# Four sums moved from the end of a run-time choice to behind it, in an attention and mixture-of-experts kernel

## The chip, the cores and the metric

The kernel runs on one core of a Trainium2 chip. The metric is the device time of one execution in microseconds (us), as a median of five runs. The engines are named as in the profile: PE is TensorE, DVE VectorE, ACT ScalarE, POOL GpSimd, SP the engine that issues most DMAs.

## The reference

Attention with 4 batches, 8 heads, 768 positions and head size 64 gives 3072 tokens of 512 numbers. A router then gives each token to one of 8 experts, and each expert applies two matrix products with a ReLU between them:

```python
logits = xn @ en.T / tau
expert_idx = np.argmax(logits, axis=1)
...
for e in range(E):
    mask = expert_idx == e
    if not mask.any():
        continue
    h = np.maximum(x[mask] @ w1[e], 0.0)          # w1[e]: 512 x 1024
    out[mask] = gate_w[mask, None] * (h @ w2[e])  # w2[e]: 1024 x 512
```

All of it is float32. How many tokens an expert gets is known only while the kernel runs.

## The kernel before

The first 190 us or so are attention and routing, which the change does not touch. After them the experts run one after the other, with a first block of 256 tokens (`n.first`) that was started earlier and ends in front of expert 0. The instructions of PE, ACT, DVE, SP and POOL are issued in the order in which the program is written (`manual_schedule`), so the place of a line in the code is its place in each engine's queue.

**The choice.** Each expert has one arm of a run-time switch per possible width (its number of tokens, rounded up to a multiple of 32). At the switch each engine jumps to the arm for the width; at the arm's end it jumps to the code that stands behind the switch and that all arms share. The widths that this input takes can be read from the matmul shapes of the trace: 160 for expert 0, then 320, 512, 320, 352, 384, 480 and 384 for experts 1 to 7. The widest arm, 512, is the last one in the code, so that its end runs straight on into the code behind the switch.

**An arm of experts 1 to 7.** `first_by_seven` makes the first product in seven smaller products of sums and differences instead of eight. For this it needs sums of the tokens (`xsum`, made by `token_sums`, lines L1039 to L1042) and of the weights w1 (`fsum`, made by `first_sums`, L1064 to L1067). The four sums of a kind have the numbers 0 to 3 in a list. Sums for the *next* expert are made on DVE while this expert runs: the first two of w1 and the first two of x between the seven products, the last two of each at the end of the arm. `making` is the list that an arm runs on DVE after its seven products: four sums of the hidden rows (`hsum`, also L1064 to L1067, 128x512), then the last two of x (L1041, L1042, 128x512) and the last two of w1 (L1066, L1067, 128x1024). Beside this PE makes second products of rows beyond the first 256 (L1219 for full tiles of 128 rows, L1232 for a part of 64 or 32).

**Behind the choice.** `choose_next` loads the width after next into registers (L1490) and gives a hint (L1496). `unfinished.pop()()` finishes the expert before: one DVE instruction (L1112; for expert 0 L1029) reads the PSUM tile `work0` and writes `y`. Then `Pair` makes the second product of the first 256 rows, again in seven smaller products of four matmuls, all at L1101. In `pair.begin` PE makes four of them, ACT copies the first (`p1`, L1121), and DVE adds: `u2` and `u3` (L1105), which ACT multiplies with the gates (L1125, L1131). In `pair.end` PE makes the rest. Its first product goes to `work0`, of which there is one, so it waits until DVE has read the old one; ACT reads it as `p5` (L1144); PE makes the `fourth` product; and only then, because it adds to the tile that ACT had to read, the last product. After this PE jumps into the next expert's arm.

```python
self.product(ps, s1, t1)                          # pair.end
nc.scalar.mul(self.p5, ps, self.gate[1])
self.plus(self.part(1, 1), self.p5, self.u3g)
self.fourth()
self.product(ps, s4, self.b[1][1], True)
```

**Weights.** SP issues the 2 MB load of w1 for expert e+2 when expert e no longer needs its own (L167), and that of w2 likewise (L168).

**Expert 0.** Its token numbers come from DRAM (`numbers`, tile `mts`), DVE casts them to integers (`cast`, tile `idss`), POOL gathers the rows with them (`gather_rows`, L985, tile `xg`), PE turns each 128 rows (`turn_row`, L1011, PSUM tile `work`, three buffers), and ACT or DVE copies them from PSUM into `xT` (L1014). Expert 0's own arm has no sums: it uses `first_by_eight` (L1262).

## Time and profile before

| | us |
|---|---|
| median of 5 runs | 523.61 |
| lowest and highest of them | 521.46, 525.12 |
| the profiled execution: time, span | 524.95, 523.2 |

| engine | busy us | share of the span |
|---|---|---|
| PE (matmul) | 497.0 | 95% |
| PEld (weight load) | 410.7 | 78% |
| DVE | 300.2 | 57% |
| ACT | 198.4 | 38% |
| POOL | 145.0 | 28% |

The span is the time from the first to the last instruction of the profiled execution; its granted TensorE clock was 0.992. In the lists below a row of the timeline gives the start in us from the span's start, the duration, the engine, the line, the operation, the tiles written and read, the count, and in brackets how long the engine was idle before and what ended that. In the chain of waits a row gives start, duration and what ran; "issue" is time in which an engine waited for nothing that the profile shows. Jumps, register loads and semaphore waits are not counted as busy, but the trace has records of them.

### The profile page before, as it was taken

To read this page: it belongs to the slowest core of one execution; us is meant where nothing else is said; L and a number is where in the kernel's file an instruction comes from. 1 tells how busy PE (TensorE), PEld (TensorE's weight loads), DVE (VectorE), ACT (ScalarE), POOL (GpSimd) and SP (SyncE) were. 2 spreads that over 40 slices of the span, in tenths; PEclk is the share of its full clock that TensorE was granted. 3 is DMA by queue.
4 is the path that set the end of the run, shared out by engine and by line. 5 is a ranking of instruction groups with operands and counts; after the bars stand their busy time and mean duration, and the time that the engine had idled before them with its cause. 6 is when DMAs were issued, how large, how long until landed. Compare 5 with 4: busy or idle time off the path is not lost.

```text
span 523.2 us, 13705 instructions
## 1 busy us (share of the span) xinstructions
PE 497.0 (95%) x5606; PEld 410.7 (78%) x5606; DVE 300.2 (57%) x597; ACT 198.4 (38%) x498; POOL 145.0 (28%) x169
## 2 busy tenths in 40 slices
PE   7999999999989799999889999999899999999994
PEld 7677787887857688779778579879799689869963
DVE  5746767766775665657535715836835734633531
ACT  4966776776644322313113212312322222311210
POOL 4221121332254335542430034042133040022031
PEclk9999999999999899999999999999999999999998
DMA  9999988899633517883570056246146423001001
GB/s 174 195 185 178 233 230 192 192 236 209 150 77 115 139 34 180 258 298 127 193 264 3 16 206 233 85 169 241 55 181 226 164 80 145 1 25 58 0 22 68
DMA packets 111422, 76.32 MB, mean 146 GB/s; under 512 B 87078, under 2 KB 95270, under 8 KB 111282
## 3 DMA queue, kind: packets, MB, share of 16 engines
q1 hardware_dynamic: 102769, 59.00, 42.2%
q0 software_dynamic: 6912, 15.26, 8.7%
q8 instruction: 63, 1.03, 0.9%
q14 instruction: 78, 0.63, 0.4%
q10 hardware_dynamic: 1600, 0.39, 0.3%
HBM read 61.66 MB, written 17.16 MB: 151 GB/s over the span
## 4 chain that ended last, share of the span: by engine, by line
PE 56%; DVE 7%; issue 5%; POOL 2%; DMA 2%; ACT 1%; DVEq 0%; POOLq 0%
PE big L1286 24%; PE big L1101 10%; PE work L1219 7%; PE work L1101 5%; PE work L1011 2%; PE pa L670 2%; PE big L1262 2%; PE work L1232 1%; PE work L1021 1%; DMA meta<-mt,slot 1%; DMA xg<-x_dram,idss 1%; POOL meta L256 1%; DVE fsum L1066 1%; POOL ss L223 1%; POOL xg L985 1%
## 5 line engine op out<-in xcount | busy, mean ns | idle before, releaser
L492 DVE TENSOR_TENSOR ex<-ex,table 126x768 f32<-126x768 f32 x64 | 60.6, 952 | 38.7 <-ACT ex L485 38.5
L1298 DVE TENSOR_TENSOR hT<-big,hT 128x320 f32<-128x320 f32 (+4 forms) x70 | 39.4, 566 | 49.7 <-PE big L1286 49.5
L1238 POOL DMA_INDIRECT out_dram<-y_arm,tids x17 | 17.9, 1051 | 166.4 <-ACT y_arm L1221 121.4
L1286 PE MATMUL big<-xT,w1t 128*128 128x160 f32 (+4 forms) x336 | 59.5, 330 | 1.6 <-issue 1.5
L485 ACT ACTIVATE ex<-pa 126x384 f32<-126x384 f32 (+1 forms) x128 | 53.3, 477 | 17.1 <-PE pa L479 16.0
L1286 PEld LDWEIGHTS big<-xT,w1t 128*128 128x128 f32 x336 | 54.1, 190 | 4.6 <-issue 2.8
L508 PE MATMUL od<-ex,v 126*64 126x192 f32 (+1 forms) x576 | 46.2, 305 | 0.4 <-DVE ex L492 0.4
L985 POOL DMA_INDIRECT xg<-x_dram,idss x32 | 32.9, 1028 | 45.1 <-PE big L1286 17.4
L508 PEld LDWEIGHTS od<-ex,v 126*64 126x64 f32 x576 | 34.6, 136 | 8.2 <-issue 3.7
L1014 ACT COPY xT<-work 128x256 f32<-128x256 f32 x60 | 19.3, 376 | 57.1 <-PE work L1011 56.7
L256 POOL DMA_INDIRECT meta<-mt,slot x24 | 27.6, 1149 | 43.9 <-DVE rd L552 21.1
L1286 PE MATMUL big<-xsum,fsum 128*128 128x160 f32 (+4 forms) x224 | 39.6, 330 | 0.0
L479 PE MATMUL pa<-qT,kT 64*32 64x128 f32 (+3 forms) x2048 | 38.1, 263 | 0.7 <-issue 0.5
L479 PEld LDWEIGHTS pa<-qT,kT 64*32 64x32 f32 (+1 forms) x2048 | 29.3, 105 | 11.9 <-issue 6.8
L1286 PEld LDWEIGHTS big<-xsum,fsum 128*128 128x128 f32 x224 | 36.1, 190 | 1.1
L1219 PE MATMUL work<-w2t,hT 128*128 128x512 f32 x80 | 35.1, 593 | 0.0
L1101 PE MATMUL big<-wsum,hsum 128*128 128x256 f32 x136 | 31.1, 380 | 0.7 <-DVE idss L1650 0.5
L1300 ACT ACTIVATE hT<-hT 128x320 f32<-128x320 f32 (+4 forms) x42 | 21.6, 533 | 25.1 <-DVE hT L1298 24.9
L429 POOL COPY v<-v 30x896 f32<-30x896 f32 (+1 forms) x15 | 16.4, 1105 | 49.2 <-DMA v<-in_v_dram 29.5
L1101 PEld LDWEIGHTS big<-wsum,hsum 128*128 128x128 f32 x136 | 25.7, 190 | 5.3 <-issue 1.0
L1101 PE MATMUL big<-w2t,hT 128*128 128x256 f32 x112 | 27.7, 385 | 1.4 <-DVE fsum L1066 1.1
L1219 PEld LDWEIGHTS work<-w2t,hT 128*128 128x128 f32 x80 | 15.1, 190 | 17.5 <-issue 17.2
(245 smaller groups left out, 873.2 us busy)
## 6 DMA issues: line engine op xcount, KB each, us to landing
w1t<-in_moe_w_dram SPq DMA_DIRECT2D x6, 2048.0 KB, 8.9
w2t<-in_moe_w_dram SPq DMA_DIRECT2D x6, 2048.0 KB, 10.0
v<-in_v_dram SPq DMA_DIRECT2D x32, 192.0 KB, 4.4
x_dram<-xs SPq DMA_DIRECT2D x23, 256.0 KB, 4.3
k<-in_k_dram SPq DMA_DIRECT2D x28, 192.0 KB, 4.7
q<-in_q_dram SPq DMA_DIRECT2D x28, 192.0 KB, 4.9
w1t<-in_moe_w_dram SPq DMA_DIRECT2D x32, 128.0 KB, 4.3
w2t<-in_moe_w_dram SPq DMA_DIRECT2D x32, 128.0 KB, 4.3
```

The lines of the kernel that those rows point to most:

```text
L256: i = nc.gpsimd.indirect_dma_start(out=k.meta[:], out_offset=bass.IndirectOffsetOnAxis(ap=slot[:, t : t + 1], axis=0), in_=mt[:, t, :], in ...
L479: i = nc.tensor.matmul(u.sp[e][k0:k1, a * n + c0 : a * n + c1], lhsT=t.kT[rows, j, k0:k1], rhs=t.qT[rows, j * BLK + c0 : j * BLK + c1], st ...
L485: nc.scalar.activation(u.ex[:, e], u.sp[e][0:ROWS, 0 : 2 * u.n].rearrange("p (a c) -> p a c", a=2), AF.Exp, scale=k.scale)
L492: nc.vector.tensor_tensor(out=exv, in0=exv, in1=tab[:, :, 0 : u.n // BLK, :], op=ALU.mult)
L508: nc.tensor.matmul(g.od[a][e * D : (e + 1) * D, at : at + c1 - c0], lhsT=g.v[0:ROWS, 2 * a + e, u.j, :], rhs=u.ex[:, e, a, c0:c1], start=f ...
L985: i = k.nc.gpsimd.indirect_dma_start(out=xg[:], out_offset=None, in_=k.x_dram[0 : upto or k.N + 1, :], in_offset=bass.IndirectOffsetOnAxis ...
L1014: copy(out=xT[:, :, a, j * half : (j + 1) * half].rearrange("p c (q i) -> p c q i", i=LACE), in_=laced(ps[:])[:, a])
L1101: self.k.nc.tensor.matmul(ps, lhsT=x[:, f, :], rhs=w[:, f, :], start=f == 0 and not add, stop=True, skip_group_check=True)
L1219: nc.tensor.matmul(ps[:], lhsT=hT[:, f, j * P : (j + 1) * P], rhs=w2[:, f, :], start=i == 0, stop=i == k.NF - 1)
L1286: nc.tensor.matmul(to[f // 2][:, f % 2 * 256 : f % 2 * 256 + h], lhsT=x[:, l, f * P : (f + 1) * P], rhs=y[:, l, 0:h], start=not (add or f ...
L1298: nc.vector.tensor_tensor(out=to, in0=x, in1=z, op=ALU.add)
L1300: nc.scalar.activation(to, to, AF.Relu)
```

## The change

It has three parts.

1. The last two sums of x and of w1 for the next expert leave the end of the arms of experts 1 to 7 (expert 7 has none, since nothing comes after it). They stand behind the switch, after the DVE instruction that finishes the expert before and ahead of `pair.begin`.
2. The turned rows of expert 0 are copied to `xT` by DVE alone. Before, ACT copied tiles 0 and 2, and DVE tiles 1 and 3.
3. The cast of expert 0's row numbers stands behind one more of the four hidden sums of the first block: behind the third instead of the second in the order in which they are issued.

```diff
@@ expert
         if now.e:
             coming.first_sums, ahead = first_sums(k, coming.w[0])
-            making += more[2:] + ahead[2:]
...
         choose_next()
         out += unfinished.pop()()
+        for make in more[2:] + ahead[2:]:
+            make()
         pair.begin()
@@ kernel
             making[1]()
             making[2]()
+            making[0]()
             cast(0, 1)
             coming = prepare(0)
             gathers = coming.gathers
-            making[0]()
             making[3]()
...
             for j in range(CAP // P):
-                turn_row(n, coming.rows, coming.xT, j, (nc.scalar.copy, nc.vector.tensor_copy)[j % 2])
+                turn_row(n, coming.rows, coming.xT, j, nc.vector.tensor_copy)
```

## The prediction

> **What bounds the kernel now.** I read the chain of waits first. By engine it says that PE sets the time:

> ```profile
> PE 56%; DVE 7%; issue 5%; POOL 2%; DMA 2%; ACT 1%; DVEq 0%; POOLq 0%
> ```

> So a change on DVE counts only where DVE or "issue" stands in the chain. I went through the experts in order of time. Behind experts 2, 4, 5 and 6 the chain is PE alone; behind experts 1 and 3 it leaves PE. This is the chain over the end of expert 1:

> ```profile
> 247.48 0.69 DVE hsum L1064
> ...
> 249.53 0.69 DVE hsum L1067
> 250.22 0.61 DVE xsum L1041
> ...
> 252.76 0.07 DVE fsum L1067
> 252.83 4.25 issue
> ...
> 257.93 0.76 DVE y L1029
> 258.69 0.04 issue
> 258.74 1.99 PE work L1101 x8
> 260.73 1.73 PE big L1101 x8
> 262.46 1.73 PE work L1101 x8
> 264.19 1.53 issue
> ```

> The reader is to see the eight sums at the arm's end, a gap of 4.25 us, then the `y` that frees `work0`, and PE behind it. The four sums that move end at 253.98 and take 3.84 us (250.14 to 253.98). The gap is DVE's jump out of the arm. The trace's record of that jump starts with the last sum, at 252.77, and the next instruction follows 4.30 us later; register work takes another 0.86 us. The list of waits prices the two places for PE:

> ```profile
> PE work L1101 <- DVE y L1029: 1.6, 1, 1.6
> PE work L1101 <- DVE y L1112: 1.3, 1, 1.3
> ```

> These 1.6 us (expert 1) and 1.3 us (expert 3) are all that an earlier `y` can give; every other gap of PE has another cause.

> Next, why the jump is long. Between its record and the next instruction, DVE's jump out of an arm took 4.30, 0.52, 4.26, 5.49, 2.87, 2.74 and 2.73 us behind experts 1 to 7; ACT's took 5.67, 0.40, 5.35, 5.63, 2.57, 2.40 and 2.55. The 0.5 belongs to the last arm, which runs straight on. The quiet price is 2.7. The long ones lie in the load of w1, issued at 248.36, 336.77 and 375.88. The stages view shows DMA share and GB/s in its last two columns:

> ```profile
> 247.00:249.00 2.00, 2.00 (x22) 1.30 (x20) 1.49 (x3) 0.45 (x1) 0.00 (x0) 1.00 0.03 8
> 250.00:251.00 1.00, 1.00 (x7) 0.90 (x6) 0.96 (x3) 0.47 (x1) 0.13 (x1) 1.00 0.87 303
> 251.00:255.00 4.00, 4.00 (x20) 3.53 (x19) 2.95 (x3) 0.00 (x0) 3.28 (x3) 1.00 1.03 421
> 256.00:258.00 2.00, 1.12 (x6) 0.64 (x4) 0.07 (x1) 0.37 (x1) 0.17 (x1) 1.00 0.04 11
> ```

> The load fills the DMA engines from 250 to 255, and the queue view of 249 to 258 has code in it:

> ```profile
> q14 instruction: 4, 0.03, 1.0%
> ```

> I read a jump as a fetch of code that comes behind the load. ACT jumps at 250.13, right as the load starts, and pays 5.67; DVE jumps at 252.77, halfway through, and pays 4.30.

> **Part 1, expert 1.** Without the four sums DVE's jump starts with its last hidden sum, at 249.53 instead of 252.77: 3.24 us earlier, but at the load's start. How long it is there the trace does not show for DVE. Bounds: 2.7 (quiet) and 5.7 (ACT, 0.6 us later in the same stage). I take 5.6, from ACT's row, as the nearest in time. Then DVE is back at 255.13, `y` starts at 255.99 (+0.86), and the sums, which now stand in front of `u2`, run from 256.66 (+0.67) to 260.50 (+3.84). `u2` started at 258.60; it is 1.90 late. PE gains first: it is free at 257.13, finds `work0` read, and no longer waits 1.6. But its last product waits for `p5`, and on ACT `p5` is queued behind the gate products of `u2` and `u3`: from `u2`'s start to `p5`'s end is 0.45 + 0.53 + 0.53 + 0.47 = 1.98 at best. So `p5` ends at 262.48; it ended at 261.24. PE's jump to expert 2 comes 0.35 after `p5` and takes 3.9 us here, past the last product (that is the 1.53 "issue" above). All 1.24 us arrive in expert 2: **+1.24**. In general `p5` ends at 256.88 plus the jump, not before 259.63 (PE's own first product), so the break-even jump is 4.36.

> **Part 1, expert 3.** The jump starts at 337.97 instead of 341.21; load issued 1.2 us before, as for expert 1. I take 5.4 (ACT here 5.35, DVE behind expert 4 5.49). Back at 343.37, `y` 344.23, sums 344.63 to 348.47, `u2` +1.75, `p5` ends 350.45. Here PE's jump is covered, so the end of `p5` counts against the last product's start at 350.58: 0.15 for the semaphore gives 350.60, so nothing, or **+0.1** with the pipeline refilled. The 1.3 us that `y` gives is eaten. Break-even jump: 5.38; PE's own products let at most 1.56 be gained.

> **Part 1, elsewhere.** Expert 4: DVE jumps at 373.95, ahead of its load; with a jump up to 6.1 `p5` still comes from PE. Expert 5: jump at 413.29, in its load; `p5` would end 420.49 plus the jump, against 426.29 now: covered up to 5.8. Experts 2 and 6: DVE idled 8.9 and 6.0 us in front of `u2`. In the built program L1042 and L1067 now also wait for PE's arm to be nearly or wholly done; for experts 2 and 6 that puts the sums' end near 307 and 467.5, before `u2` at 309.36 and 469.97. Zero for all four; without that cover up to 2.4 us each. What needs the sums, the next arm's second product, is over 5 us away. The scatters on POOL only move earlier. [...]

> **Part 2.** Four more DVE copies of 0.38 us and four fewer on ACT. These rows show the place, with part 3's cast and gather:

> ```profile
> 195.39 0.17 DVE L1650 CAST idss<-mts 128x8 int32<-128x8 f32 x1
> 195.47 0.68 DVE L1064 TENSOR_TENSOR hsum<-fhT 128x512 f32<-128x512 f32 x1
> ...
> 195.83 1.19 POOL L985 DMA_INDIRECT xg<-x_dram,idss  x1 [7.72 <-DVE idss L1650]
> ...
> 204.59 0.63 PE L1011 MATMUL work<-ident,xg 128*128 128x128 f32 x4 [0.53 <-DMA xg<-x_dram,idss]
> ```

> DVE is free at 203.33, after a step of the first block, and would copy tiles 0 to 2 by 205.6; PE needs tiles 0 and 1 for expert 0's 160 columns, at 205.60, and tile 0's buffer for the last turning. Tiles 0 and 1 are there at 204.85. DVE's following small steps move by some 0.4 us; it idles 4.97 before the next row that PE's result ends (224.03). **Zero**; at most 0.4 if the cover were gone.

> **Part 3.** The title says three sums; in the built order the cast passes one, L1064, which takes DVE 0.60 us (195.47 to 196.07). POOL had waited for this cast, each gather moves with it, and PE waits 0.53 for the last one. Behind it PE runs through to expert 1 without a break, so **+0.60** arrives. The bound below is 0: the numbers had landed just when the cast ran, and in an execution where they land 0.6 later the sum costs nothing. The sums that passed the cast were not waited for.

> **The sum.** 1.24 + 0.1 + 0.60 = +1.94. Against the profiled 524.95 (span 523.2 and 1.75 around it) this is 526.9; that execution lay 1.34 above the median, so against 523.61 it is **525.6**, or +0.4%. About 0.5%, 2.6 us, is what a measurement of this kernel can tell from no change: my forecast is a small loss inside it.

> **Rival B, not slower: the fetch stays ahead of the load.** At 249.53 and 337.97 the DMA share is still below full (0.29 in 249 to 250). With today's 4.3 us `p5` ends 0.06 earlier at expert 1 and PE's last product starts 1.12 earlier at expert 3: -1.18 + 0.60 = -0.6, or 523.0. With the quiet 2.7 both stages gain what PE allows, 1.61 and 1.56: -3.17 + 0.60, or 521.0. For it: DVE jumps 0.6 us before ACT. Against it: ACT jumped 0.45 us after the load's issue at expert 4, earlier than DVE would (1.2), and paid 5.63.

> **Rival C, slower: the load, not the jump's start, sets when code arrives.** If DVE comes back no earlier than today (257.07, 345.47), `p5` ends 3.2 later at expert 1 and PE's last product starts 2.1 later at expert 3: +5.3 + 0.60, or 529.5. Every us beyond the jumps I took costs 2 us, so half of that mechanism gives 527.5; from jumps 0.35 us longer than taken it is a loss that can be told. For it: DVE's fetch would stand beside ACT's, and the three jumps near 5.5 end when the load is mostly through. Against it: ACT came back at 255.80, earlier than DVE, in the same load.

> **Chances.** The forecast 0.6, with its own range 524.4 to 526.8 (jumps of 5.2 to 5.9, the cast 0 to 0.6); B 0.16; C 0.24. Over 526.2 lie C and about a third of the forecast: slower 0.44. Under 521.0 lies the far end of B: 0.05. Within: 0.51. The range takes in most of B and the half of C: 522.2 to 528.0.

> **What would show it.** Behind experts 1 and 3 DVE's jump starts with L1067 of `hsum` and lasts over 5 us; PE no longer waits for `y`, but for `p5` on ACT, by 1 us or more; L1286 of expert 2 starts later by 1.2 relative to expert 1's start. The last gather of expert 0 lands 0.6 later, and PE's wait for it grows to about 1.1. Jumps under 4.4 and 5.4 would prove B, jumps over 6 C. A new wait behind experts 2, 4, 5 or 6 would make the covers wrong.

## The result and the profile after

The changed kernel takes 525.86 us (median of 39 runs; 522.39 to 528.70) against 523.25 for the kernel before (65 runs). The ratio is 1.0047, with an interval of 1.0035 to 1.0058: a loss of about 2.5 us, small but clear of no change. The forecast was 525.6. The two kernels were compared once more later, where the ratio was 1.0030 (1.0005 to 1.0056).

The profiled execution of the changed kernel took 523.99 us, with a span of 522.2 and a clock of 0.989. It is shorter than that of before, and this has nothing to do with the change: its attention part, which both kernels share, ended 2.1 us earlier (first hidden sum at 191.90 instead of 194.04). From the first hidden sum to the end it took 330.28 us against 329.20, so +1.08. For this reason stages are compared here, not spans. A stage runs from one expert's first product to the next one's; "front" runs from the first hidden sum to expert 0's first product. "Again" is a second profiled execution, from the later comparison, us:

| | front | 0 | 1 | 2 | 3 | 4 | 5 | 6 | 7 | end |
|---|---|---|---|---|---|---|---|---|---|---|
| before | 11.56 | 23.60 | 36.51 | 52.01 | 34.43 | 37.79 | 39.14 | 49.26 | 37.66 | 7.24 |
| before, again | 11.62 | 24.47 | 37.68 | 52.01 | 34.49 | 38.08 | 39.14 | 49.26 | 37.66 | 7.22 |
| after | 12.12 | 23.20 | 37.48 | 52.01 | 34.48 | 37.54 | 39.14 | 49.26 | 37.66 | 7.39 |
| after, again | 12.20 | 24.85 | 37.93 | 52.01 | 34.62 | 37.94 | 39.14 | 49.26 | 37.66 | 7.44 |

Of the +1.08, front brings +0.56, expert 1 +0.97, expert 0 -0.40, expert 4 -0.25, and the rest +0.20.

The list of waits of the kernel after, PE's part from 185 us on, shows the exchange (us in total, times, longest):

```profile
PE work L1101 <- ACT ptmp L1144: 3.3, 2, 1.9
PE work L1011 <- DMA xg<-x_dram,idss: 1.0, 1, 1.0
```

No wait for `y` is left. In its place stand two waits for `p5`, 1.9 behind expert 1 and 1.4 behind expert 3, where the waits for `y` had been 1.6 and 1.3. This is the timeline of the same two places:

```profile
247.47 0.69 DVE L1067 TENSOR_TENSOR hsum<-hT,hsum 128x512 f32<-128x512 f32 x1
254.28 0.75 DVE L1029 TENSOR_SCALAR y<-work,mts 128x512 f32<-128x512 f32 x1 [6.11 <-issue]
254.94 0.68 DVE L1041 TENSOR_TENSOR xsum<-xT 128x512 f32<-128x512 f32 x1
...
257.66 1.22 DVE L1067 TENSOR_TENSOR fsum<-w1t,fsum 128x1024 f32<-128x1024 f32 x1
258.80 0.94 DVE L1105 TENSOR_TENSOR ptmp<-big,ptmp 128x256 f32<-128x256 f32 x2
...
349.36 1.99 PE L1101 MATMUL work<-w2t,hsum 128*128 128x256 f32 x8 [1.36 <-ACT ptmp L1144]
```

DVE leaves the arm right behind its last hidden sum, as the change wants, and then stands idle for 6.11 us. The `y` it returns with is in time; but the four sums now come before `u2` (the row at 258.80), and ACT can make `p5` only behind `u2`. The chain of waits of the kernel after shows where that goes:

```profile
255.08 1.99 PE work L1101 x8
257.07 1.74 PE big L1101 x8
258.81 0.41 DVE ptmp L1105
...
260.19 0.47 ACT ptmp L1144
260.66 0.04 issue
260.70 3.26 PE work L1101 x8
263.96 0.74 issue
264.70 5.42 PE big L1286 x24
```

PE makes its first product as soon as it can, stops, and the chain leaves it for DVE (`u2`) and ACT (`p5`). The windows of DMA traffic (last two columns: DMA share and GB/s) show that the whole jump, from 247.49 to 253.42, lies within the load of w1, which was issued at 246.30 and whose packets run from 247.34 to 254.32:

```profile
249.00:250.00 1.00, 1.00 (x7) 0.87 (x6) 0.00 (x0) 0.00 (x0) 0.83 (x1) 1.00 0.99 410
250.00:255.00 5.00, 5.00 (x24) 4.12 (x22) 0.72 (x2) 0.37 (x1) 2.96 (x3) 1.00 0.77 296
255.00:257.00 2.00, 1.98 (x10) 1.72 (x10) 1.90 (x4) 0.00 (x0) 1.18 (x1) 1.00 0.00 0
```

### The profile page after: what moved, and what is told of

It is laid out like the page before. It is cut to its first block, busy times and chain, and to the rows that moved or that the text cites. A ratio compares the mean times of both kernels' runs of the same rounds, so it can differ in the third digit from the quotient of the medians.

```text
span 522.2 us, 13718 instructions
## 1 busy us (share of the span) xinstructions
PE 498.6 (95%) x5606; PEld 411.3 (79%) x5606; DVE 301.9 (58%) x601; ACT 196.8 (38%) x494; POOL 147.3 (28%) x169
## 3 DMA queue, kind: packets, MB, share of 16 engines
q8 instruction: 63, 1.03, 0.8%
## 4 chain that ended last, share of the span: by engine, by line
PE 82%; DVE 5%; ACT 5%; DMA 3%; issue 2%; POOL 2%; POOLq 0%; SPq 0%; ACTq 0%; DVEq 0%
PE big L1286 25%; PE big L1101 12%; PE work L1219 7%; PE od L508 6%; PE work L1101 5%; PE pa L479 5%; PE work L1232 4%; PE pa L454 3%; PE od L518 3%; PE work L1011 2%; PE pa L670 2%; ACT ex L485 2%; PE big L1262 2%; PE pa L581 1%; PE work L1021 1%
## 5 line engine op out<-in xcount | busy, mean ns | idle before, releaser
L1286 PE MATMUL big<-xT,w1t 128*128 128x160 f32 (+4 forms) x336 | 59.4, 330 | 0.7 <-issue 0.7
L1286 PEld LDWEIGHTS big<-xT,w1t 128*128 128x128 f32 x336 | 54.2, 190 | 3.8 <-issue 1.9
L985 POOL DMA_INDIRECT xg<-x_dram,idss x32 | 33.8, 1055 | 44.1 <-PE big L1286 22.8
L1286 PE MATMUL big<-xsum,fsum 128*128 128x160 f32 (+4 forms) x224 | 39.6, 330 | 0.0
L1014 ACT COPY xT<-work 128x256 f32<-128x256 f32 x56 | 18.0, 376 | 55.7 <-PE work L1011 55.3
L1286 PEld LDWEIGHTS big<-xsum,fsum 128*128 128x128 f32 x224 | 36.1, 190 | 1.1
L1101 PE MATMUL big<-wsum,hsum 128*128 128x256 f32 x136 | 31.1, 380 | 0.5 <-ACT ptmp L1121 0.5
L1101 PEld LDWEIGHTS big<-wsum,hsum 128*128 128x128 f32 x136 | 25.7, 190 | 5.1 <-ACT ptmp L1121 0.9
L1101 PE MATMUL big<-w2t,hT 128*128 128x256 f32 x112 | 27.7, 385 | 1.1 <-ACT y L1234 1.1
```

The costliest lines, as they stand in the source:

```text
L985: i = k.nc.gpsimd.indirect_dma_start(out=xg[:], out_offset=None, in_=k.x_dram[0 : upto or k.N + 1, :], in_offset=bass.IndirectOffsetOnAxis ...
L1101: self.k.nc.tensor.matmul(ps, lhsT=x[:, f, :], rhs=w[:, f, :], start=f == 0 and not add, stop=True, skip_group_check=True)
L1286: nc.tensor.matmul(to[f // 2][:, f % 2 * 256 : f % 2 * 256 + h], lhsT=x[:, l, f * P : (f + 1) * P], rhs=y[:, l, 0:h], start=not (add or f ...
```

## The experiments

**Each part by itself.** Three kernels, each with one part of the change, and one that moves the sums one step further, behind `pair.begin`, so that `u2` comes before them. The edit of the last:

```diff
-            making += more[2:] + ahead[2:]
...
         pair.begin()
+        for make in more[2:] + ahead[2:]:
+            make()
```

Part 1 alone:

> Part 1 alone: the four sums behind the choice, the rest as before. Theory of the prediction (DVE's jump meets the load of w1, and the sums then stand in front of u2 and so of p5): jumps of 5.2 to 5.9 us behind experts 1 and 3, expert 1's stage (its first matmul to expert 2's) +1.0 to +1.25, expert 3's within 0.1, all others 0; time +1.1 to +1.4. Rival (the earlier y wins): jumps under 4.4, time -1 or less. Rival (the moved code itself costs elsewhere, by the layout of DVE's code or by the new waits for PE): other stages grow, time +2 or more.

Part 2 alone:

> Part 2 alone: DVE copies all four of expert 0's turned tiles. Theory: 0.0, PE starts expert 0's first product no later, since tiles 0 and 1 are copied before it is free. Rival (one engine is too slow for four tiles): expert 0's first product starts up to 0.4 later and the time is +0.4. Rival (ACT freed of its copies helps expert 0): the stage of expert 0 is 0.4 shorter, as in the one profile after the change.

Part 3 alone:

> Part 3 alone: the cast of expert 0's row numbers behind one more sum. Theory: +0.6, and PE waits about 1.1 instead of 0.5 us for the last gather of expert 0. Rival (the row numbers land later than the cast in most executions): 0.

Sums behind `pair.begin`:

> The kernel before, with the four sums moved one step further: behind pair.begin, so that y and u2, u3 both come ahead of them. If p5 behind the sums is what eats the gain, then here PE waits neither for y nor for p5: expert 1's stage -1.3 to -1.6 and expert 3's -1.3 to -1.5, time -2.5 to -3.1. Rival (the sums have to be early because the next arm needs them, or DVE's jump into it comes late): PE waits in the next arm instead, and the time is 0 to +2.

Measured, as ratios to the kernel before: part 1 alone 1.0073 (1.0042 to 1.0104), part 2 alone 0.9978 (0.9949 to 1.0008), part 3 alone 0.9996 (0.9967 to 1.0026), sums behind `pair.begin` 0.9929 (0.9893 to 0.9965). So the loss belongs to part 1. It lost some 3.9 us alone, more than the +1.1 to +1.4 of its theory: experts 1 and 3 took 1.16 and 0.18 more, about as expected, but expert 0 took 26.97 instead of 23.60, which is the sign that the second rival had named (taken up again under what stays open). It is not the jump alone that makes the loss: with the same early and long jumps (5.79 and 5.56 us) but `u2` ahead of the sums, the kernel is faster than with part 1 and faster than before. Its stages for experts 1 and 3 took 34.35 and 32.86 us, 2.16 and 1.57 less than before; for expert 1 that is more than the 1.3 to 1.6 expected, because PE's jump into expert 2 came 1.8 earlier, counted from expert 1's start, and took 3.56 us instead of 3.92. The sum, 3.73, is as large as the measured gain (0.71% of 531.45 is 3.8), though front and expert 0 were 2.95 longer in this trace than in that of before. The timeline of this kernel at expert 3 is the counterpart of the one above:

```profile
349.15 0.48 DVE L1112 SCALAR_TENSOR_TENSOR y<-work,mts,u2g 128x256 f32<-128x256 f32 x1 [5.74 <-DMA out_dram<-y_arm,tids]
350.24 0.95 DVE L1105 TENSOR_TENSOR ptmp<-big,ptmp 128x256 f32<-128x256 f32 x2 [0.61 <-issue]
```

`u2` starts 1.1 us after `y`, and PE waits neither for the `y` that frees `work0` nor for `p5`. What is late next is expert 2's first product. PE's list of waits names the adding of the last `y` (L1105), which is now queued behind the sums on DVE; but that `y` ends at 269.75, while PE's own jump, begun at 266.68, has its next instruction at 270.25. So it is PE's jump that holds PE up here, not DVE.

```profile
PE big L1286 <- DVE y L1105: 1.2, 1, 1.2
```

**The two kernels again, half of the move, and the load.** Then came both kernels once more, a kernel in which only the sums of w1 stand behind `pair.begin` and those of x in front of it, and the kernel after with its two loads of weights in the other order, so that w1's load is not under way when DVE jumps:

```diff
         out += unfinished.pop()()
+        for make in more[2:]:
+            make()
         pair.begin()
+        for make in ahead[2:]:
+            make()
```

```diff
-    nc.sync.dma_start(w[0][:], k.w1[e].rearrange("(c p) f -> p c f", p=P))
...
+    nc.sync.dma_start(w[0][:], k.w1[e].rearrange("(c p) f -> p c f", p=P))
```

The kernel before, again:

> The kernel before once more, for a second trace of it: 0.0 against itself. It tells how far the stages that no part touches (attention, expert 0) move between executions of one kernel. If expert 0's stage here also lies near 25 to 27 us instead of 23.6, its spread is no effect of any part; if it stays at 23.6, part 1 has a cost in expert 0 that the prediction missed.

The kernel after, again:

> The changed kernel once more, beside the kernel before on the same chip. By the prediction's terms +1.9 (stages: first block +0.6, expert 1 +1.0 to +1.25, expert 3 +0.1, rest 0). If the price lies elsewhere as well, over +3, and a stage outside these three is longer in both traces of it.

Half of the move:

> The kernel before with the two x sums (1.4 us) behind the choice ahead of pair.begin, as in part 1, but the two w1 sums (2.4 us) behind pair.begin. If what stands in front of u2 is charged to p5 us for us, expert 1's stage is 2.4 shorter than in part 1 alone, down to PE's own limit: -0.9 to -1.6 against before, expert 3's -1.3 to -1.6, time -2.2 to -3.1. If instead merely having sums between y and u2 is what costs, it stands near part 1 alone, at +1.

The loads exchanged:

> The changed kernel, with each later expert's load of w2 issued ahead of that of w1, so that no load runs while DVE and ACT jump out of an arm. If the load is what makes the jumps long: DVE's jumps behind experts 1, 3 and 5 take 2.7 to 3.0 us instead of 5.9, 5.4 and 5.4, and ACT's behind 1, 3 and 4 take 2.4 to 2.8 instead of 5.5 to 5.7; PE's wait for p5 behind experts 1 and 3 is then gone. If the place in the code is what makes them long, they stay over 5. The time itself is no test: w1 comes some 15 us later, and the sums of it may have to wait.

The kernel before came out at 1.0000 (0.9970 to 1.0029) and the kernel after at 1.0030 (1.0005 to 1.0056). Expert 0 took 24.47 us in the kernel before, between the two values that were to tell something: its stage moves by 0.9 without any change, but 25 to 27 was not reached.

Half of the move came out at 0.9939 (0.9911 to 0.9966), with jumps of 6.02 and 5.40 us. Its timeline behind expert 1:

```profile
258.99 0.75 DVE L1029 TENSOR_SCALAR y<-work,mts 128x512 f32<-128x512 f32 x1 [6.20 <-issue]
...
261.06 0.94 DVE L1105 TENSOR_TENSOR ptmp<-big,ptmp 128x256 f32<-128x256 f32 x2
...
263.35 1.89 PE L1101 MATMUL work<-w2t,hsum 128*128 128x256 f32 x8
```

From `y` to `u2` it is 2.07 us here, against 4.52 in the kernel after (254.28 to 258.80). In the trace `p5` ends at 262.90, before PE wants it at 263.35: no wait for `p5`, and the stages of experts 1 and 3 are 35.14 and 32.86, that is 1.37 and 1.57 shorter than before. Against part 1 alone (37.67 and 34.61), 2.4 us of DVE work in front of `u2` are thus worth 2.53 and 1.75 at these two places, 4.3 us in all. The ratios lie further apart, 0.6 to 0.7% slower and 0.6% faster; expert 0 differs as well (26.97 and 27.96 against 25.23).

The kernel with the loads exchanged settles why the jump is long. Its timeline, and PE's list of waits:

```profile
262.74 0.75 DVE L1029 TENSOR_SCALAR y<-work,mts 128x512 f32<-128x512 f32 x1 [3.12 <-issue]
```

```profile
PE big L1286 <- DVE hT L1298: 12.6, 4, 6.1
```

No wait for `p5` is left on PE. The gap in front of `y`, 6.11 us in the kernel after, is 3.12 with the same code at the same place. Behind experts 1, 3 and 5 DVE's jump took 2.94, 2.78 and 2.72 us instead of 5.93, 5.37 and 5.35, and ACT's behind experts 1, 3 and 4 took 2.63, 2.75 and 2.51 instead of 5.71, 5.48 and 5.52. The time of this kernel (540.66 in a single run) says nothing about the jump, since w1 now comes late and the first sums of w1 hold up the arm: that is the 12.6 us of the second fence. The jump's length is thus shown to come from the load.

What the jump waits for can be seen in the queue that carries code. These are lines of the queue view of the kernel after: the first for 247.49 to 251.4, where no packet of code starts, the second for 251.4 to 253.5.

```profile
q1 hardware_dynamic: 318, 1.30, 91.3%
q14 instruction: 2, 0.02, 1.9%
```

The two packets have 8 KB of code each. The first starts at 251.47, 3.98 us after DVE's jump, and DVE's next instruction comes 1.95 later. With the loads exchanged a packet starts 1.00 us after the jump, and the next instruction comes 1.94 later. In every trace, DVE is back 1.8 to 2.0 us after the start of a packet of code behind experts 1 and 3 to 6. So what the load adds is some 3 us of waiting in front of the packet (3.98 against 1.00).

**Repeats, and the best version with part 2.** The effects were small against their intervals, so parts 1 and 3 and the sums behind `pair.begin` ran again, the last also together with part 2:

> Part 1 alone once more, since its first interval (+0.42% to +1.04%) lies above the stages that its trace shows (+1.2 and +0.2 us, some 0.25%). Theory: +1.3 us, that is a ratio of about 1.0025; the first ratio was high by the spread of expert 0's stage and attention. Rival (part 1 has a price that no stage of the trace shows): again over 1.004.

> Part 3 alone once more. The cast itself has stood 0.60 later in every trace with it. Theory: up to +0.6, less where the row numbers or the gather land late: a ratio of 1.0 to 1.0012, and the first interval (0.9967 to 1.0026) narrows around that. Rival: a ratio under 0.999, if the later gathers meet less traffic.

> The four sums behind pair.begin once more: -3.7 us by its two stages (-2.2 and -1.6), a ratio of 0.993, as in the first run. If the first ratio was luck: 0.997 or more.

> The four sums behind pair.begin, with part 2 (DVE alone copies expert 0's tiles). If part 2 is worth nothing, as its trace says, this equals the run without it within 0.2%. Rival (the first ratio of part 2, 0.998, was real): 1 us faster than the run without it.

Part 1 alone came out at 1.0059 (1.0033 to 1.0086), over 1.004 as its rival said, part 3 alone at 1.0004 (0.9985 to 1.0024), the sums behind `pair.begin` at 0.9923 (0.9893 to 0.9954), and the same with part 2 at 0.9923 (0.9898 to 0.9948). Part 2 adds nothing there, and part 3 is worth nothing that can be measured. The move behind `pair.begin` is the version to keep, 0.7 to 0.8% faster than the kernel before; the part of it that counts is that `u2` stands ahead of the sums.

## Why the prediction was right, point by point

**The number (right, in part by luck).** The forecast of 525.6 lies 0.3 from the measured 525.86, but its terms are not that good one by one. Part 1 was put at +1.34 and lost 3 to 4 us when it stood alone; part 2 was put at 0 and came out 1.2 faster, with an interval that holds 0; part 3 was put at +0.60 and came out at 0, with an interval that holds both. The three ratios multiply to the 1.0047 of the whole, so errors of both signs met in the sum. What the traces of the whole change do bear out is the mechanism at the two places that the prediction worked through.

**The jump (right).** The prediction read the jump as a fetch of code behind the 2 MB load of w1, and took 5.6 us at expert 1 and 5.4 at expert 3; the kernel after has 5.93 and 5.37 (again: 5.81 and 5.51). The loads exchanged show that the load is the cause (2.94 and 2.78 there), and the packets of code that the wait is for them: DVE is back 1.95 us after the start of one with the load, and 1.94 after it without. A jump of DVE out of an arm to other code thus took 2.7 to 2.9 us without a load under way and 5.4 to 5.9 with one just issued, of which some 3 us are the wait of the code behind the load.

**Expert 1 (right; two terms off against each other).** The prediction had +1.24, the stage shows +0.97. The jump was 0.33 longer than taken, so that `u2` came 2.26 later than before, not 1.90, counted from the last hidden sum. From `u2` to the end of `p5` it took 1.86 instead of 1.98. And PE's jump into expert 2 took 3.51 us, not the 3.92 of the trace before: 1.24 + 0.33 - 0.12 - 0.41 is 1.04. That the errors of the three terms cancel is luck. The second pair of executions shows +0.25 only, because the kernel before has a loss of its own there, told below.

**Expert 3 (right).** +0.1 forecast, +0.05 and +0.13 seen. The wait for `p5` was 1.36. The 0.15 that the prediction took for the semaphore was an estimate; the rows come to as much only with PE's restart in it: 0.05 us from the end of `p5` to the first matmul (349.31 to 349.36 in the kernel after; 346.81 to 346.86 behind `y` in the kernel before), and 0.10 in front of the second, which follows after 0.32 us where the later ones follow after 0.22.

**Elsewhere (right).** Experts 2, 5 and 6 have the same stages in all four executions, and expert 4 took 0.25 and 0.14 less than in its partner, not more: the covers held, with jumps of 5.35 and 5.88 behind expert 5, where the cover was said to reach to 5.8. The move also took DVE's jump behind expert 4 out of its load (2.76 us instead of 5.49) and that behind expert 5 into one (5.35 instead of 2.87). One reading of the prediction was too simple: at the end of expert 4 the chain of waits is not PE alone, but runs over DVE's sums, and PE's list has a wait of 1.1 us there for a sum that moves (`fsum`, L1066). With the sum gone the wait is as long, 1.1, and stands under ACT's `y` (L1234), so the sum was not its cause.

**Rivals.** B (the jump keeps to 4.3 or less) is refuted by the 5.93. C (DVE comes back no earlier than today) is refuted too: counted from the last hidden sum, `y` starts at 6.81 in the kernel after and started at 8.40 in the kernel before, so 1.6 earlier.

**Part 2 (zero in the sum; one thing not seen).** The measured -0.22% has an interval that holds 0, and with the sums behind `pair.begin` it changed nothing. But the traces show an effect in expert 0 that the prediction did not look for. Where ACT still copies tiles 0 and 2, it jumps into expert 0's arm only after its last copy, into the loads of parts of w2: in the kernel before the jump lasts from 204.28 to 208.31, and eight of the 16 loads of 128 KB are issued within it, from 204.59 on; in the kernel after it lasts from 199.56 to 203.80, and two are issued by then. Without part 2 its first ReLU came between 1.7 and 7.0 us after expert 0's first product, in nine executions; with part 2 it came after 1.4 to 1.5 in all five. In the two executions with part 1 alone it came after 5.3 and 7.0, and PE waited 1.1 and 2.8 us for it. So part 2 moves that jump ahead of most of these loads. For the second execution of part 1 alone, these are the list of waits, and the windows:

```profile
PE big L1262 <- ACT hT L1264: 2.8, 1, 2.8
```

```profile
200.00:204.00 4.00, 4.00 (x21) 3.51 (x20) 0.78 (x2) 1.21 (x3) 3.08 (x4) 1.00 0.73 176
216.00:220.00 4.00, 4.00 (x21) 3.96 (x20) 3.69 (x8) 0.79 (x3) 3.39 (x3) 0.60 0.92 263
```

The first number after the brackets of POOL is the granted clock. It is 1.00 in 200 to 204, in front of expert 0, and 0.60 in 216 to 220, behind the wait of 2.8.

**Part 3 (mechanism right, size taken at its upper end).** The cast came 1.93 us after the first hidden sum instead of 1.35, as forecast, and front took 0.56 and 0.58 more in the two pairs; PE's wait for the last gather was 1.02 (1.1 forecast). But when it stood alone the part came out at 0.9996 and 1.0004, where +0.60 would be 1.0011: its intervals hold both that and zero. A likely reason, not shown, is in the traces of kernels with the old order: their front took 11.56 to 12.59 us, so it moves by 1 us from one execution to another without the part, and may take in some of the 0.6.

**What stays open.** Part 1 alone lost 0.59 to 0.73%, 3 to 4 us; its two profiled executions show +1.16 and +1.05 in expert 1 and +0.18 and +0.13 in expert 3. The remainder lies elsewhere: expert 0 took 26.97 and 27.96 us, against 23.6 to 25.8 in the other kernels without part 2, and in the second execution expert 2 took 53.69 instead of 52.01, because the clock was halved behind a gap of 2.52 us (below). ACT's late jump is one cause in expert 0, but not the whole of it: with the sums behind `pair.begin` the first ReLU came after 5.0 and 5.5, and expert 0 took only 25.5 and 24.8 us. The jump is late there because ACT's third copy is: it starts 1.8 and 3.2 us after PE has turned its rows with part 1 alone, 2.2 and 2.0 with the sums behind `pair.begin`, and 0.04 in both executions of the kernel before. What it waits for, the traces do not show. Part 1 changes no instruction of ACT. Whether the moved code changes how that jump meets the loads, or these executions fell badly, was not settled; nor was why the changed kernel's first ratio, 2.5 us, is larger than the +1.1 and +1.4 by which its two profiled executions are longer from the first hidden sum on (the later ratio, 1.0030, is 1.6 us).

## What to carry to other kernels

An instruction moved earlier gains only up to the next thing that is late: here `y` came earlier, and the work that was put between it and `u2` cost the same consumer more, one step later; ask for each moved piece which of the two results around it the bound engine wants sooner. The length of a jump is not a constant: look for bulk loads under way at the moment where it will stand after the change (here DVE's took 2.7 to 2.9 us without a load and 5.4 to 5.9 with one just issued). Where one engine has slack only behind a certain point, put the filler work behind the last result that another engine waits for, not behind the first.

## What the runs showed of the hardware that was not expected

**A wait of 1.9 us can cost PE's clock.** In the second execution of the kernel before, PE waited 1.89 us for `y`, where it had been 1.6 in the first. This is its timeline, and then the same 2 us in the windows of this execution and of the first one:

```profile
261.12 3.05 PE L1101 MATMUL work<-wsum,hsum 128*128 128x256 f32 x8 [1.89 <-DVE y L1029]
```

```profile
262.00:264.00 2.00, 2.00 (x7) 1.53 (x6) 0.48 (x1) 0.47 (x1) 0.32 (x1) 0.50 0.34 131
```

```profile
262.00:264.00 2.00, 2.00 (x11) 1.58 (x9) 0.00 (x0) 0.47 (x1) 0.96 (x1) 1.00 0.28 98
```

The eight matmuls took 3.05 us instead of 1.99, at a granted clock of 0.50 instead of 1.00; by the trace's records of the clock the slow stretch lasted 3.41 us. That is the main reason why the stage of expert 1 took 37.68 there and not 36.51. Of the eleven gaps of PE of 1.89 us and more that stand behind the first hidden sum, eight halved the clock: the one above, 1.90 for `p5` behind expert 1 in both executions of the kernel after (3.26 us for the last product in the chain shown, hidden under PE's jump), 1.96 for `y` in a trace of part 3 alone (expert 3 took 36.77 instead of 34.43), 2.52 and 2.81 in one of part 1 alone, 3.37 and 6.11 with the loads exchanged. Three did not: 1.91, 2.25 and 2.33.

Less than 2 us of idleness in one such window was thus enough. So a wait near 1.9 us had a cliff beside it here, 1.06 us for the eight matmuls above, and the kernels that leave the four sums in the arm, with waits for `y` of 1.61, 1.89, 1.68, 1.59 and 1.82 behind expert 1, stood at its edge. The sums behind `pair.begin` take those waits away.
